# Reordering the opening of a fused conv and MLP kernel: half 1's conv shared differently between TensorE and VectorE, casts and transposes moved, a load held back

## The chip, the cores and the metric

One core of a Trainium2 chip runs the kernel. The metric is the device time of one execution in microseconds (us); lower is better. The kernel before took 698.84 us (median of 3, 698.34 to 699.54).

## The reference, cut to what matters

```python
# _attn_ref: x (8, 4096, 192), weight (8, 7)
w = softmax(weight, axis=-1)                       # 8 heads of 24 channels, 7 taps
out[b, s, h, g] = sum_k w[h, k] * x_pad[b, s + k, h, g]     # causal conv over the sequence
# _moe_ref: 32768 tokens
h = x @ w_in                                       # 192 -> 2048
g = np.maximum(0.01 * h, h)
return g @ w_out                                   # 2048 -> 192
```

## The kernel before

The tokens go through in blocks of 512 positions of two sequences. The first five blocks (NHALF) are done as two halves of 256 positions, the others whole. For each half: the conv makes `yt` (three chunks of 64 channels for both sequences), the first product `ph` is computed in units of two PSUM banks, ScalarE's leaky relu empties a unit into `g`, and the second product `po` follows a half later. The conv normally runs on VectorE, one multiply and six multiply-adds a chunk. At the start, when TensorE has nothing else to do, it does some chunks with diagonal matrices (`pe_conv_jobs`, 28 matmuls a chunk).

The first two blocks (halves 0 to 3) come by plain loads (`load_first`, float32), a cast, transposes on TensorE into PSUM and copies into `xt`. From block 2 on, casting loads and DMA transposes do this (`load_x`, `transpose_x`).

```python
    def cast_first(q, e, copy): ...        # x_nat -> x_bf, on the engine that is passed
    def transpose_first(q): ...            # 12 transposes on TensorE into two "po" PSUM buffers
    def evac_first(q, *copies): ...        # PSUM -> xt
    def conv_jobs(grp, chunks): ...        # VectorE: 7 instructions a chunk
    def pe_conv_jobs(grp, c): ...          # TensorE: 28 matmuls, and a scaling that empties them
    def mm1(grp, u): ...                   # one unit of ph, and its activation on ScalarE
```

The loop, with the opening's special cases:

```python
        for j in range(steps):
            for u in range(2 * j, 2 * j + 2):
                mm1(grp, u)
                if i == 0 and u == 1:
                    transpose_first(1)
                    evac_first(1, nc.vector.tensor_copy, nc.vector.tensor_copy)
                    ahead = conv_jobs(groups[1], range(NPEC, NCH))       # NPEC = 2
                    ...                                                  # two chunks for TensorE
                if i == 0 and u == 2:
                    for e in range(2):
                        cast_first(2, e, nc.scalar.copy)
                if i == 0 and u == 4:
                    transpose_first(2)
                    evacs[0](act_scale)
                if i == 0 and u in (3, 5):
                    for job in pe_ahead[: 4 * K]:
                        job()
                    ...
            for _ in range(quota):
                mm2_slot(slot)                                           # po
                slot += 1
            ...
```

Of the kernel before, what the change touches and what calls it, by code (L numbers as in the profile page):

```python
# [9 lines left out]
FP32 = mybir.dt.float32  # L10
BF16 = mybir.dt.bfloat16
# [3 lines left out]
def kernel(  # L15
# [8 lines left out]
    nc = tc.nc  # L24

    B, S, D = x.shape
    H, K = weight.shape
# [8 lines left out]
    NCH = D // CH  # L36
    ST = 512
    SUB = ST // 128
    HT = ST // 2
    HS = SUB // 2  # L40
    NFC = F // 128
# [5 lines left out]
    NPEC = 2  # L47
# [22 lines left out]
    def load_x(blk):  # L70

        if blk >= NBLK:
            return
        rp, st = divmod(blk, NB)
        t = xb_pool.tile([128, NCH, SUB, 2, CH], BF16, name="x_bf")
        src = x[:, st * ST : (st + 1) * ST, :].rearrange("r (s p) d -> r p s d", p=128)
        for c in range(NCH):
            for e in range(2):
                nc.gpsimd.dma_start(  # L79
                    out=t[:, c, :, e, :],  # L80
                    in_=src[2 * rp + e, :, :, c * CH : (c + 1) * CH],
                )
        x_bf[blk] = t

    def transpose_x(blk):

        if blk >= NBLK:
            return
        rp, st = divmod(blk, NB)
        if st == 0:  # L90
            new_xt(rp)
        t = x_bf.pop(blk)
        for c in range(NCH):
            nc.sync.dma_start_transpose(
                out=xt[rp][:, c, HALO + st * ST : HALO + (st + 1) * ST].rearrange(
                    "p (s k) -> p s k", s=SUB
                ),
                in_=t[:, c, :, :, :].rearrange("p s e k -> p (s e k)"),
            )
# [7 lines left out]
    def load_first(q, after=None):  # L107
        t = stage_pool.tile([128, 2, HS, D], FP32, name="x_nat")
        for e in range(2):
            ins = nc.sync.dma_start(  # L110
                out=t[:, e, :, :],
                in_=x[e, q * HT : (q + 1) * HT, :].rearrange("(c p) d -> p c d", p=128),
            )
            if after is not None and e == 0:
                tc.add_manual_dep(
                    ins.ins, after.ins.name,
                    mybir.DependencyInfo(
                        mybir.DependencyClass.Sync, mybir.DependencyReason.DATA
                    ),
                    reason="leave the DMA engines to w_in",  # L120
                )
        x_nat[q] = t

    def cast_first(q, e, copy):
        if q % 2 == 0 and e == 0:
            x_bf[q // 2] = xb_pool.tile([128, NCH, SUB, 2, CH], BF16, name="x_bf")
        h = q % 2
        copy(  # L128
            out=x_bf[q // 2][:, :, h * HS : (h + 1) * HS, e, :],
            in_=x_nat[q][:, e, :, :].rearrange("p s (c k) -> p c s k", c=NCH),  # L130
        )
# [20 lines left out]
    def evac_first(q, *copies):  # L152
        dst = xt[0][:, :, HALO + q * HT : HALO + (q + 1) * HT].rearrange(
            "p c (s i k) -> p i s c k", s=HS, i=2
        )
        for i, t in enumerate(ptr.pop(q)):
            copies[i](out=dst[:, i], in_=t)  # L157
# [4 lines left out]
    def conv_jobs(grp, chunks=range(NCH)):  # L162
        blk, t0, T = grp
        rp, st = divmod(blk, NB)
        if blk not in yt:
            yt[blk] = yt_pool.tile([128, NCH, ST], BF16, name="yt")
        y = yt[blk]
        jobs = []
        for c in chunks:
            for k in range(K):  # L170
                a = BASE + k + st * ST + t0
                src = xt[rp][:, c, a : a + T]
                dst = y[:, c, t0 : t0 + T]
                if k == 0:
                    jobs.append(
                        lambda s=src, d=dst, c=c: nc.vector.tensor_scalar_mul(  # L176
                            d, s, wk[:, c, 0:1]
                        )
                    )
                else:  # L180
                    jobs.append(
                        lambda s=src, d=dst, c=c, k=k: nc.vector.scalar_tensor_tensor(  # L182
                            out=d, in0=s, scalar=wk[:, c, k : k + 1], in1=d,
                            op0=mybir.AluOpType.mult, op1=mybir.AluOpType.add,
                        )
                    )
        return jobs
# [60 lines left out]
    def warm(n):  # L248
        for _ in range(n):
            nc.tensor.matmul(  # L250
                out=wa[:, 0, 0:HT], lhsT=zero[:, 0:128], rhs=zero, start=True, stop=True
            )
# [9 lines left out]
        out=w9[:, 0:K], in_=w9[:, 0:K], func=mybir.ActivationFunctionType.Exp,  # L262
        bias=nmax, scale=1.0, accum_out=w9[:, K : K + 1],
    )
    warm(7)
    wps = psum_h.tile([128, 2, ST], FP32, name="wps", tag="ph")
    for c in range(NCH):
        nc.tensor.matmul(  # L268
# [7 lines left out]
    cast_first(0, 1, nc.scalar.copy)  # L276

    wraw = wps[:, 0, 0 : NCH * (K + 1)].rearrange("p (c k) -> p c k", c=NCH)
    wkh = const_pool.tile([128, NCH, K], BF16, name="wkh")
    wkl = const_pool.tile([128, NCH, K], FP32, name="wkl")  # L280
    nc.vector.tensor_copy(out=wkh, in_=wraw[:, :, 0:K])
    nc.vector.tensor_sub(wkl, wraw[:, :, 0:K], wkh)


    diag = [const_pool.tile([128, 2, K, CH], BF16, name=f"diag{c}") for c in range(NPEC)]
# [14 lines left out]
        return act  # L300

    transpose_first(0)
    warm(3)
    diag_high(0)
    diag_low(0, range(2))
    evac_first(0, nc.vector.tensor_copy, nc.scalar.copy)
# [12 lines left out]
        )  # L319

    load_first(2, low)
    for job in conv_jobs(groups[0], range(NPEC, NCH)):
        job()
    for c in range(NPEC):
        pe_jobs, evac_y = pe_conv_jobs(groups[0], c)
        for job in pe_jobs:
            job()
        evac_y(act_scale)
        warm(3)
    cast_first(1, 0, nc.vector.tensor_copy)  # L330
    cast_first(1, 1, nc.vector.tensor_copy)
    load_first(3)
    load_x(2)
    transpose_x(2)


    g, po, osb, seal = {}, {}, {}, {}
# [70 lines left out]
    def evac_o(n):  # L408
# [7 lines left out]
        if n % 2 == 1:  # L416
# [3 lines left out]
                in_=osb.pop(n // 2),  # L420
            )

    slot, avail = 0, 0
    for i, grp in enumerate(groups):
        blk, t0, T = grp
        steps = T // 64
        if t0 == 0:
            g[blk] = g_pool.tile([128, NFC, 2, ST], BF16, name="g", tag="g")
        quota = (avail - slot) // steps

        if i == 0:
            ahead, pe_ahead = [], []
        elif i == 1:
            ahead = early[4:]
        else:
            ahead = conv_jobs(groups[i + 1]) if i + 1 < len(groups) else []
        per = -(-len(ahead) // (steps - 1)) if T == ST else -(-len(ahead) // steps)
        for j in range(steps):
            for u in range(2 * j, 2 * j + 2):
                mm1(grp, u)  # L440
                if i == 0 and u == 1:
                    transpose_first(1)
                    evac_first(1, nc.vector.tensor_copy, nc.vector.tensor_copy)
                    ahead = conv_jobs(groups[1], range(NPEC, NCH))
                    evacs = []
                    for c in range(NPEC):
                        pe_jobs, evac_y = pe_conv_jobs(groups[1], c)
                        pe_ahead += pe_jobs
                        evacs.append(evac_y)
                    per = len(ahead)  # L450
                if i == 0 and u == 2:
                    for e in range(2):
                        cast_first(2, e, nc.scalar.copy)
                if i == 0 and u == 4:
                    transpose_first(2)
                    evacs[0](act_scale)
                if i == 0 and u in (3, 5):
                    for job in pe_ahead[: 4 * K]:
                        job()
                    pe_ahead = pe_ahead[4 * K :]  # L460
                if i == 1 and u in (0, 2):
                    cast_first(3, u // 2, nc.scalar.copy)
            for _ in range(quota):
                mm2_slot(slot)
                slot += 1
            if i == 0 and j == 3:
                evac_first(2, nc.vector.tensor_copy, nc.vector.tensor_copy)
                early = conv_jobs(groups[2])
                for job in early[:4]:
                    job()  # L470
                evacs[1](nc.vector.tensor_scalar_mul)
            for job in ahead[per * j : per * (j + 1)]:
                job()
            if i == 1 and j == 1:
                transpose_first(3)
            if i == 1 and j == 3:
                evac_first(3, nc.vector.tensor_copy, nc.vector.tensor_copy)

            last_half = t0 + T == ST
            if j == steps // 4 and last_half:  # L480
                load_x(blk + 3)
            if j == steps // 2 and last_half and blk > 0:
                transpose_x(blk + 2)
        avail += 2 * T // 128 * NFC
# [37 lines left out]
```

## Time and profile before

| | kernel before |
|---|---|
| time | 698.84 us |
| span of the profiled execution | 696.4 us |
| TensorE (PE) busy | 689.5 us, 99% |
| VectorE (DVE), ScalarE (ACT) busy | 538.2 us, 513.3 us |
| first po matmul, from the span's start | 24.41 us |

A kernel whose TensorE is 99% busy can gain only where TensorE isn't in its steady beat, and that is the first 24 us. The prediction shows the lines.

### The profile page before, as it was taken

How to read it: one execution, taken by the hardware profiler on the slowest of the kernel's cores; microseconds unless marked ns; L12 is line 12 of the kernel's file. 1: busy time of each engine (PE TensorE's matmuls, PEld its weight loads, DVE VectorE, ACT ScalarE, POOL GpSimd, SP SyncE). 2: the span in 40 equal slices, each digit the busy share in tenths (PEclk: the TensorE clock that was granted, in tenths of full speed). 3: DMA queues.
4: the chain of work that ended last, by engine and by line, in shares of the span. 5: the costliest groups of instructions: out<-in, count | busy, mean ns of one | idle time of the engine just before them, and what ended most of it. 6: DMA issues, size and time to landing. Idle time of an engine off the chain costs nothing.

```text
span 696.4 us, 26058 instructions
## 1 busy us (share of the span) xinstructions
PE 689.5 (99%) x11786; PEld 612.7 (88%) x11786; DVE 538.2 (77%) x991; ACT 513.3 (74%) x579; POOL 142.1 (20%) x198
## 2 busy tenths in 40 slices
PE   8999999999999999999999999999999999999997
PEld 6899999678888888888888888888888888888887
DVE  6899999768777788777787777787777787777712
ACT  6888888977777777777777777777777777777770
POOL 6342221320122220222220222211222220000000
PEclk9999999999999999999999999999999999999999
DMA  9986553853556545556545556645556644122112
GB/s 173 127 98 76 82 80 77 88 78 73 76 65 92 82 70 81 74 66 93 81 69 81 73 69 93 79 67 85 66 76 88 86 71 72 53 52 59 47 37 69
DMA packets 184847, 54.39 MB, mean 78 GB/s; under 512 B 148384, under 2 KB 184736, under 8 KB 184736
## 3 DMA queue, kind: packets, MB, share of 16 engines
q0 software_dynamic: 98768, 14.17, 29.7%
q1 hardware_dynamic: 85968, 38.56, 23.1%
q8 instruction: 92, 1.51, 0.9%
q14 instruction: 19, 0.16, 0.1%
HBM read 29.88 MB, written 25.17 MB: 79 GB/s over the span
## 4 chain that ended last, share of the span: by engine, by line
PE 97%; DMA 1%; ACT 1%; POOL 0%; issue 0%; DVE 0%; SPq 0%; POOLq 0%; ACTq 0%
PE po L376 49%; PE ph L356 47%; DMA x_nat<-in_x_dram 1%; ACT g L363 1%; PE acc L201 0%; PE wps L268 0%; ACT diag L296 0%; POOL sel L228 0%; PE warm L250 0%; PE ptr L143 0%; ACT x_bf L128 0%; ACT xt L157 0%; POOL sel L226 0%; DVE o_sb L415 0%; POOL ident masks.py:199 0%
## 5 line engine op out<-in xcount | busy, mean ns | idle before, releaser
L363 ACT ACTIVATE g<-ph 128x1024 bf16<-128x1024 f32 x512 | 496.5, 1021 | 161.0 <-PE ph L356 161.0
L182 DVE SCALAR_TENSOR_TENSOR yt<-xt,wk,yt 128x512 bf16<-128x512 bf16 (+1 forms) x642 | 439.7, 685 | 17.4
L376 PE MATMUL po<-w_out,g 64*128 64x192 bf16 (+1 forms) x8048 | 398.1, 243 | 0.1
L376 PEld LDWEIGHTS <-g 64*128 64x128 bf16 (+1 forms) x8048 | 372.2, 94 | 28.8 <-ACT g L363 0.4
L356 PE MATMUL ph<-yt,w_in 64*128 64x512 bf16 (+1 forms) x3552 | 391.8, 347 | 1.6 <-ACT g L363 1.3
L356 PEld LDWEIGHTS <-w_in 64*128 64x128 bf16 x3552 | 249.9, 94 | 46.1 <-issue 5.0
L79 POOL DMA_DIRECT2D x_bf<-in_x_dram x180 | 133.7, 773 | 431.0 <-DMA xt<-x_bf 422.9
L415 DVE COPY o_sb<-po 128x192 f32<-128x192 f32 x216 | 77.2, 358 | 129.5 <-PE po L376 127.2
L176 DVE TENSOR_SCALAR yt<-xt,wk 128x512 bf16<-128x512 bf16 (+1 forms) x107 | 35.9, 336 | 1.0 <-DMA xt<-x_bf 0.8
L415 ACT COPY o_sb<-po 128x192 f32<-128x192 f32 x40 | 13.1, 327 | 0.0
L201 PE MATMUL acc<-xt,diag 64*64 64x256 bf16 x112 | 7.3, 280 | 0.0
L201 PEld LDWEIGHTS <-diag 64*64 64x64 bf16 x112 | 6.0, 111 | 1.2 <-issue 0.6
L250 PE MATMUL warm<-zero 128*128 128x256 bf16 x20 | 4.5, 373 | 1.1 <-DVE junk L218 1.1
L128 ACT CAST x_bf<-x_nat 128x384 bf16<-128x384 f32 x5 | 2.5, 507 | 3.6 <-DMA x_nat<-in_x_dram 3.6
L238 POOL DMA_DIRECT2D w_in<-in_moe_w_in_dram x8 | 5.1, 643 | 0.0
L157 DVE COPY xt<-ptr 128x384 bf16<-128x384 bf16 x7 | 2.2, 352 | 2.8 <-PE ptr L143 2.8
L250 PEld LDWEIGHTS <-zero 128*128 128x128 bf16 x20 | 2.0, 122 | 2.2 <-DVE junk L218 1.1
L296 ACT ACTIVATE diag<-ident,wkl 128x64 bf16<-128x64 bf16 x14 | 3.6, 339 | 0.0
L128 DVE CAST x_bf<-x_nat 128x384 bf16<-128x384 f32 x3 | 1.2, 439 | 1.4 <-DMA x_nat<-in_x_dram 1.4
L317 ACT ACTIVATE yt<-acc,rsum 128x256 bf16<-128x256 f32 x3 | 1.4, 470 | 1.2 <-PE acc L201 1.2
L143 PEld LDWEIGHTS <-x_bf 64*128 64x128 bf16 x48 | 1.2, 101 | 1.0 <-ACT x_bf L128 1.0
L268 PEld LDWEIGHTS wps<-w,sel 8*128 8x128 f32 x6 | 1.4, 322 | 0.7 <-POOL sel L228 0.7
(28 smaller groups left out, 12.5 us busy)
## 6 DMA issues: line engine op xcount, KB each, us to landing
out_dram<-o_sb SPq DMA_DIRECT2D x128, 192.0 KB, 2.1
x_bf<-in_x_dram POOLq DMA_DIRECT2D x180, 64.0 KB, 3.3
x_nat<-in_x_dram SPq DMA_DIRECT2D x8, 192.0 KB, 5.8
w_in<-in_moe_w_in_dram POOLq DMA_DIRECT2D x8, 192.0 KB, 7.8
xt<-x_bf SPq DMA_TRANSPOSE x90, 2.5
w_out<-in_moe_w_out_dram POOLq DMA_DIRECT2D x1, 768.0 KB, 14.2
w<-in_weight_dram SPq DMA_DIRECT2D x1, 0.2 KB
```

The costliest lines, as they stand in the source:

```text
L79: nc.gpsimd.dma_start(out=t[:, c, :, e, :], in_=src[2 * rp + e, :, :, c * CH : (c + 1) * CH],)
L128: copy(out=x_bf[q // 2][:, :, h * HS : (h + 1) * HS, e, :], in_=x_nat[q][:, e, :, :].rearrange("p s (c k) -> p c s k", c=NCH),)
L176: lambda s=src, d=dst, c=c: nc.vector.tensor_scalar_mul(d, s, wk[:, c, 0:1])
L182: lambda s=src, d=dst, c=c, k=k: nc.vector.scalar_tensor_tensor(out=d, in0=s, scalar=wk[:, c, k : k + 1], in1=d, op0=mybir.AluOpType.mult, ...
L201: lambda k=k, p=p, a=a, e=e, ps=ps: nc.tensor.matmul(out=acc[ps, :T], lhsT=diag[c][ps, p, k, :], rhs=xt[0][ps, c, a : a + T], start=(k == ...
L238: nc.gpsimd.dma_start(out=w_in[e * CH : (e + 1) * CH, :, fs], in_=moe_w_in[:, fs].rearrange("(c p) f -> p c f", p=CH),)
L250: nc.tensor.matmul(out=wa[:, 0, 0:HT], lhsT=zero[:, 0:128], rhs=zero, start=True, stop=True)
L296: act = nc.scalar.activation(out=diag[c][:, 1, k, :], in_=ident2, func=mybir.ActivationFunctionType.Copy, scale=wkl[:, c, k : k + 1],)
L356: nc.tensor.matmul(out=ph[:, e, i * T : (i + 1) * T], lhsT=w_in[ps, c, f * 128 : (f + 1) * 128], rhs=y[ps, c, t0 : t0 + T], start=(c == 0) ...
L363: act = nc.scalar.activation(out=g[blk][:, nf * u : nf * (u + 1), :, t0 : t0 + T], in_=ph.rearrange("p e (i t) -> p i e t", i=nf), func=my ...
L376: ins = nc.tensor.matmul(out=po[m], lhsT=g[b][ps, fc, e, s * 128 : (s + 1) * 128], rhs=w_out[ps, fc, :], start=(rt != 1 and fc == 0), stop ...
L415: copy(out=o_sb[:, n % 2, :], in_=po.pop(n))
```

## The change

The intent: take work off TensorE and ScalarE in half 0's row of units, where they hold each other up, and keep the DMA engines free for the weights. Half 1's conv goes one chunk to TensorE and two to VectorE; half 1's casts and transposes come ahead of the first ph matmul; half 2's casts go from ScalarE to VectorE and its transposes behind the eighth unit; half 3's copies come two steps earlier; block 2's loads wait for the end of half 0. The diff, cut (warm-up counts, shapes of two small tiles and removed lines are left out where `# ...` stands):

```diff
-    for job in conv_jobs(groups[0], range(NPEC, NCH)):
+    for n, job in enumerate(conv_jobs(groups[0], range(NPEC, NCH))):
+        if n in (4, 5):
+            cast_first(1, n - 4, nc.vector.tensor_copy)
         job()
+    load_first(3)
 # ...
-    cast_first(1, 0, nc.vector.tensor_copy)
-    cast_first(1, 1, nc.vector.tensor_copy)
-    load_first(3)
-    load_x(2)
-    transpose_x(2)
+    transpose_first(1)
+    evac_first(1, nc.vector.tensor_copy, nc.vector.tensor_copy)
 # ... in the loop:
+                if i == 0 and u == 0:
+                    pe_ahead, evac_y = pe_conv_jobs(groups[1], 0)
+                    ahead = conv_jobs(groups[1], range(1, NCH))
-                if i == 0 and u == 2:
-                    for e in range(2):
-                        cast_first(2, e, nc.scalar.copy)
-                if i == 0 and u == 4:
-                    transpose_first(2)
-                    evacs[0](act_scale)
-                if i == 0 and u in (3, 5):
-                    for job in pe_ahead[: 4 * K]:
+                if i == 0 and u == 3:
+                    for job in pe_ahead:
                         job()
 # ...
             if i == 0 and j == 3:
+                evac_y(nc.vector.tensor_scalar_mul)
+                for e in range(2):
+                    cast_first(2, e, nc.vector.tensor_copy)
+                transpose_first(2)
                 evac_first(2, nc.vector.tensor_copy, nc.vector.tensor_copy)
-                early = conv_jobs(groups[2])
-                for job in early[:4]:
-                    job()
-                evacs[1](nc.vector.tensor_scalar_mul)
+            if i == 1 and j == 1:
+                nc.gpsimd.tensor_copy(out=pjunk, in_=g[0][0:1, NFC - 1, 1, HT - 1 : HT])
+                load_x(2)
+            if i == 2 and j == 1:
+                transpose_x(2)
 # ...
             if i == 1 and j == 1:
                 transpose_first(3)
-            if i == 1 and j == 3:
                 evac_first(3, nc.vector.tensor_copy, nc.vector.tensor_copy)
```

More of the change, by code (lines that the diff above doesn't have):

```diff
@@ L264 @@
     )
-    warm(7)
+    warm(8)
     wps = psum_h.tile([128, 2, ST], FP32, name="wps", tag="ph")
@@ L278 @@
     wraw = wps[:, 0, 0 : NCH * (K + 1)].rearrange("p (c k) -> p c k", c=NCH)
-    wkh = const_pool.tile([128, NCH, K], BF16, name="wkh")
-    wkl = const_pool.tile([128, NCH, K], FP32, name="wkl")
-    nc.vector.tensor_copy(out=wkh, in_=wraw[:, :, 0:K])
-    nc.vector.tensor_sub(wkl, wraw[:, :, 0:K], wkh)
+    wkh = const_pool.tile([128, NPEC, K], BF16, name="wkh")
+    wkl = const_pool.tile([128, NPEC, K], FP32, name="wkl")
+    nc.vector.tensor_copy(out=wkh, in_=wraw[:, 0:NPEC, 0:K])
+    nc.vector.tensor_sub(wkl, wraw[:, 0:NPEC, 0:K], wkh)
     diag = [const_pool.tile([128, 2, K, CH], BF16, name=f"diag{c}") for c in range(NPEC)]
@@ L302 @@
     transpose_first(0)
-    warm(3)
+    warm(4)
     diag_high(0)
@@ L328 @@
         evac_y(act_scale)
-        warm(3)
-    cast_first(1, 0, nc.vector.tensor_copy)
-    cast_first(1, 1, nc.vector.tensor_copy)
-    load_first(3)
-    load_x(2)
-    transpose_x(2)
+        if c == 0:
+            warm(2)
+    transpose_first(1)
+    evac_first(1, nc.vector.tensor_copy, nc.vector.tensor_copy)
     g, po, osb, seal = {}, {}, {}, {}
@@ L421, in evac_o @@
             )
+    pjunk = const_pool.tile([1, 1], BF16)
     slot, avail = 0, 0
@@ L431 @@
         if i == 0:
-            ahead, pe_ahead = [], []
-        elif i == 1:
-            ahead = early[4:]
+            ahead = []
         else:
@@ L440 @@
                 mm1(grp, u)
-                if i == 0 and u == 1:
-                    transpose_first(1)
-                    evac_first(1, nc.vector.tensor_copy, nc.vector.tensor_copy)
-                    ahead = conv_jobs(groups[1], range(NPEC, NCH))
-                    evacs = []
-                    for c in range(NPEC):
-                        pe_jobs, evac_y = pe_conv_jobs(groups[1], c)
-                        pe_ahead += pe_jobs
-                        evacs.append(evac_y)
-                    per = len(ahead)
-                if i == 0 and u == 2:
-                    for e in range(2):
-                        cast_first(2, e, nc.scalar.copy)
-                if i == 0 and u == 4:
-                    transpose_first(2)
-                    evacs[0](act_scale)
-                if i == 0 and u in (3, 5):
-                    for job in pe_ahead[: 4 * K]:
+                if i == 0 and u == 0:
+                    pe_ahead, evac_y = pe_conv_jobs(groups[1], 0)
+                    ahead = conv_jobs(groups[1], range(1, NCH))
+                    per = len(ahead)
+                if i == 0 and u == 3:
+                    for job in pe_ahead:
                         job()
-                    pe_ahead = pe_ahead[4 * K :]
                 if i == 1 and u in (0, 2):
```

## The prediction

> **What bounds the kernel now.** I read the page's engine rows first, then the chain that ended last, then the timelines of the first 35 us engine by engine, because the diff touches nothing after the first three half blocks.
>
> ```profile
> PE 689.5 (99%) x11786; PEld 612.7 (88%) x11786; DVE 538.2 (77%) x991; ACT 513.3 (74%) x579; POOL 142.1 (20%) x198
> PE po L376 49%; PE ph L356 47%; DMA x_nat<-in_x_dram 1%; ACT g L363 1%; PE acc L201 0%; PE wps L268 0%; ACT diag L296 0%; POOL sel L228 0%; PE warm L250 0%; PE ptr L143 0%; ACT x_bf L128 0%; ACT xt L157 0%; POOL sel L226 0%; DVE o_sb L415 0%; POOL ident masks.py:199 0%
> ```
>
> TensorE (PE) is the bound: 99% busy, and 96% of the chain is the two products, ph (first) and po (second). From about 24 us on its timeline is one unbroken beat (24 ph matmuls, 32 po matmuls, 2.63 us a step). The change leaves these alone, so it can only move the moment at which the beat begins. That moment is the first po matmul, at 24.41 us:
>
> ```profile
> 10.67 0.50 PE L250 MATMUL warm<-zero 128*128 128x256 bf16 x3
> 11.11 1.58 PE L356 MATMUL ph<-yt,w_in 64*128 64x256 bf16 x24
> 12.51 0.35 PE L143 MATMUL ptr<-ident,x_bf 64*128 64x64 bf16 x12
> 13.14 1.75 PE L356 MATMUL ph<-yt,w_in 64*128 64x256 bf16 x24 [0.28 <-ACT g L363]
> 14.82 1.72 PE L201 MATMUL acc<-xt,diag 64*64 64x256 bf16 x28
> 16.47 0.83 PE L356 MATMUL ph<-yt,w_in 64*128 64x256 bf16 x12
> 17.57 0.35 PE L143 MATMUL ptr<-ident,x_bf 64*128 64x64 bf16 x12 [0.27 <-ACT x_bf L128]
> 18.48 0.83 PE L356 MATMUL ph<-yt,w_in 64*128 64x256 bf16 x12 [0.57 <-ACT g L363]
> 19.25 1.72 PE L201 MATMUL acc<-xt,diag 64*64 64x256 bf16 x28
> 20.90 1.48 PE L356 MATMUL ph<-yt,w_in 64*128 64x256 bf16 x24
> 22.85 1.75 PE L356 MATMUL ph<-yt,w_in 64*128 64x256 bf16 x24 [0.46 <-ACT g L363]
> 24.41 1.32 PE L376 MATMUL po<-w_out,g 64*128 64x192 bf16 x14
> ```
>
> Columns are start, length, engine, line. Between 11.11 and 22.85 PE does half 0's eight ph units (12 matmuls each), two transposes (ptr) and both conv chunks of half 1 (acc). The reader is to see that the units come in a halting row, although one takes only 0.66 us. Each is emptied by a ScalarE (ACT) activation of 1.02 us, and there are two ph buffers, so ACT sets the pace, and ACT is held up:
>
> ```profile
> 14.93 0.50 ACT L128 CAST x_bf<-x_nat 128x384 bf16<-128x384 f32 x1
> 17.00 0.51 ACT L128 CAST x_bf<-x_nat 128x384 bf16<-128x384 f32 x1 [1.57 <-DMA x_nat<-in_x_dram]
> 17.42 1.93 ACT L363 ACTIVATE g<-ph 128x1024 bf16<-128x1024 f32 x2
> 21.77 2.96 ACT L363 ACTIVATE g<-ph 128x1024 bf16<-128x1024 f32 x3 [1.15 <-PE ph L356]
> ```
>
> Half 2's two casts stand in ACT's order ahead of the fourth activation; the second waits 1.57 us for its load. The fourth activation, whose matmuls were issued by about 14.7, starts at 17.42. Later ACT waits 1.15 us for PE, which is then in the second conv chunk.
>
> **What the skill says.** "Perfetto Trace Analysis", section "Optimization Strategy", says to find the gaps on the bounding engine within a regime and ask which semaphore ends each; the reading above is that, and both gaps of 0.57 and 0.46 us end on ACT. "DMA: Bandwidth & Descriptors", section "Queues, rings and completion order", says that each DMA engine consumes the descriptors of a ring in order, and its section "Issuing engines are not separate DMA queues" that all issuers share the same 16 engines. The trace agrees: w_out was issued at 9.29 and took 14.2 us to land, at 23.5, behind the w_in copies (the last issued at 7.35, 11.3 us to landing, so 18.6), and the x copy waiting on its semaphore was released only then:
>
> ```profile
> 9.29 1.20 POOL L243 DMA_DIRECT2D w_out<-in_moe_w_out_dram x1 [1.31 <-DMA w_in<-in_moe_w_in_dram]
> 23.79 3.71 POOL L79 DMA_DIRECT2D x_bf<-in_x_dram x5 [3.88 <-DMA w_out<-in_moe_w_out_dram]
> ```
>
> "TensorE: Matmul & The Clock Gate", section "What's actually happening", says that the array runs at half clock until about 3.4 us of activity. The warm matmuls show it: seven take 1.67 us at 1.13, three take 0.50 at 8.58, although the clock row reads 9 throughout.
>
> **The change, part by part.**
>
> *Warm matmuls.* +1, +1, and 3+3 becomes 2. The eighth fits ahead of 3.00, where PE waits for POOL anyway. The fourth after the transposes delays the first conv by about 0.1 us (one cold matmul is 0.21, part of which comes back as warm ones later), and one fewer between the convs returns 0.11 (three take 0.33 start to start). Sum about 0.
>
> *Half 1's casts on VectorE (DVE), earlier.* They go between its conv steps from 7.70; a step is 0.52 start to start, a cast about 0.35 to 0.42. Half 1's loads have landed (in the kernel before, the casts at 10.71 show no wait). Casts done at about 10.3, DVE's chunk at 11.2 instead of 10.8. PE's second conv ends at about 10.6, transposes follow at once (0.3 us), and the first ph group needs chunk 1, which ACT delivers at 11.26 as before. So the first activation stays at about 12.1.
>
> *Transposes out of the ph row.* 0.35 us leave a place where PE waited for ACT anyway: no gain of its own.
>
> *Half 2's casts off ACT, onto DVE.* This removes the 1.57 us wait and two times 0.5 us from ACT. The fourth activation follows the third at 15.0 instead of 17.4.
>
> *One conv chunk of half 1 off PE.* 28 matmuls, 1.65 us start to start. It goes to DVE, where a chunk costs 3.4 us (13.54 to 16.95). DVE then does 11.2 copies, 11.9 and 15.2 two chunks, 18.5 scaling, 18.9 casts, done at 19.7. Half 2's transposes come after the eighth unit, on PE at about 20.1, so this fits.
>
> *The row.* Units 0 to 3 as now; conv 14.82; unit 4 at 16.47; unit 5 behind it at 17.1; unit 6 at 18.65, when unit 4 is emptied and the last w_in copy is in; unit 7 at 19.5; transposes 20.1; half 1's unit 0 at 20.7 and unit 1 at 21.65. PE would be ready for po at 22.3 instead of 24.41: 2.1 us.
>
> *w_out.* The first po needs it, and it landed at 23.5. The deferred x loads stood behind it in the ring, so taking them away moves it little, and x_nat moves the same bytes ahead of it. Then po starts at about 23.5 and the gain is 24.41 - 23.55 = 0.86 us. The other 1.2 us turn into a wait for w_out. Some DMA engines start x copies before the last w_out packet is through, so I allow 0.1 to 0.2 us for a quieter finish: 1.0 us.
>
> *DVE after that.* Half 2's conv (21 steps, 10.0 us, formerly begun at 18.6) now begins at 21.4; after 12 steps it waits for half 3's transposes (27.5), copies, and ends at about 32.9. PE needs it at 33.85 - 1.0 + 0.2 = 33.05. It just fits, and thereafter DVE needs 10.0 us a half against PE's 10.5.
>
> *Block 2's load and transposes.* Now gated on the end of half 0 and issued at about 39; needed by DVE at about 43; in the kernel before the first such transpose landed 4.5 us after issue under full load. Tight, behind a margin of 1 us.
>
> Sum: 698.84 - 1.0 = 697.9 us.
>
> **The rivals.**
>
> 1. *The whole 2.1 us arrive* (696.7). For: removing traffic might pull w_out in. Against: the ring order above; and DVE's half 2 conv, ending no earlier than about 32.5, would cap the gain near 1.5 (697.3).
> 2. *DVE becomes the bound of halves 2 and 3.* It takes on 3.4 us of conv and 0.8 of casts just where it has no slack. If its chain runs 0.5 us longer than I count, PE waits at 33; late transposes of block 2 would make it wait at 43. Cost up to 1 us: 698.8. For: margin only 0.1 to 0.3 us at 33; against: 0.5 us more slack with every half.
> 3. *Nothing changes*, because w_out slips: 698.8. Against: its bytes and its place in the ring are the same.
>
> **Range and chances.** All rivals lie between 696.7 and 699; runs of the kernel before spread over 1.2 us. I take 696.8 to 699.0. Two per cent is 14 us, more than the whole opening could give: faster 0.005, same 0.99, slower 0.005.
>
> **What would show it.** PE's longest wait turns from ACT into the w_out copy, 1 us or so just ahead of the first po, at about 23.5; ACT's activations of half 0 run without casts, the eighth over by about 21.6; half 1's first ph unit at about 20.7; half 2's first at about 32.9, with DVE's last step just before it. I am wrong if po starts well before 23 (w_out was helped), or if new DVE waits stand ahead of ph near 33 or 43.

## More of the kernel before

In the timeline of VectorE in the kernel before (start, length, engine, line, operation, count, and in brackets the idle time ahead of it and what ended it):

```profile
17.95 0.62 DVE L157 COPY xt<-ptr 128x384 bf16<-128x384 bf16 x2 [1.00 <-PE ptr L143]
18.61 0.29 DVE L176 TENSOR_SCALAR yt<-xt,wk 128x256 bf16<-128x256 bf16 x1
...
110.72 4.69 DVE L182 SCALAR_TENSOR_TENSOR yt<-xt,wk,yt 128x512 bf16<-128x512 bf16 x6
116.16 0.35 DVE L176 TENSOR_SCALAR yt<-xt,wk 128x512 bf16<-128x512 bf16 x1 [0.75 <-DMA xt<-x_bf]
```

Half 2's conv begins at 18.61. The last multiply-add of block 5, the first whole block, ends at 115.41 (110.72 + 4.69), and TensorE begins that block at 118.01:

```profile
118.01 1.48 PE L356 MATMUL ph<-yt,w_in 64*128 64x512 bf16 x12
```

VectorE is ahead: it then waits 0.75 us for a transpose of the next block.

## The result, and the profile after

The changed kernel took 698.31 us (median of 4, 698.09 to 698.45) against 698.78 (698.34 to 699.54) of the kernel before beside it; the ratio is 0.9992, 95% interval 0.9974 to 1.0009. A second set of five gave 699.01 (697.43 to 699.39) against 698.85 (698.04 to 699.34): 0.9996, interval 0.9984 to 1.0008. The two are the same within what can be told. (A ratio is the mean time of one kernel's runs over that of the other's of the same rounds, so not quite the ratio of the medians quoted.)

TensorE's timeline of the changed kernel, from the first ph matmuls on, and the one later line in which it stood still:

```profile
12.04 0.27 PE L357 MATMUL ph<-yt,w_in 64*128 64x256 bf16 x2
12.49 1.38 PE L357 MATMUL ph<-yt,w_in 64*128 64x256 bf16 x22 [0.18 <-ACT yt L317]
14.32 1.75 PE L357 MATMUL ph<-yt,w_in 64*128 64x256 bf16 x24 [0.46 <-ACT g L364]
16.00 1.72 PE L201 MATMUL acc<-xt,diag 64*64 64x256 bf16 x28
17.65 1.48 PE L357 MATMUL ph<-yt,w_in 64*128 64x256 bf16 x24
19.59 1.75 PE L357 MATMUL ph<-yt,w_in 64*128 64x256 bf16 x24 [0.46 <-ACT g L364]
21.16 0.35 PE L143 MATMUL ptr<-ident,x_bf 64*128 64x64 bf16 x12
21.54 1.75 PE L357 MATMUL ph<-yt,w_in 64*128 64x256 bf16 x24
23.99 1.31 PE L377 MATMUL po<-w_out,g 64*128 64x192 bf16 x14 [0.70 <-DMA w_out<-in_moe_w_out_dram]
...
118.99 1.04 PE L357 MATMUL ph<-yt,w_in 64*128 64x512 bf16 x8 [0.83 <-DVE yt L182]
```

The row of units now runs in pairs, and ScalarE's activations follow one another. TensorE is ready for po at 23.29 (23.99 - 0.70) although the row began 0.9 us later than before (12.04 against 11.11), and then waits for w_out. That is a gain of 0.42 us at the first po (24.41 - 23.99). At 118.99 it stands still once more: the first whole block waits 0.83 us for VectorE's conv. Matmul by matmul, TensorE is 0.49 us ahead of the kernel before until this point and 0.55 us behind after it. Two lines of the page of the changed kernel, the chain that ended last by engine and by line, say where the end now hangs:

```profile
PE 83%; DVE 12%; DMA 3%; issue 1%; POOL 0%; ACT 0%; POOLq 0%; ACTq 0%
PE po L377 43%; PE ph L357 40%; DVE yt L182 11%; DMA w_out<-in_moe_w_out_dram 2%; DVE yt L176 1%; DMA w_in<-in_moe_w_in_dram 1%; POOL sel L228 0%; ACT g L364 0%; DVE xt L157 0%; POOL sel L226 0%; DVE o_sb L416 0%; POOL ident masks.py:199 0%; PE ptr L143 0%; POOL ident masks.py:197 0%; POOLq masks.py:199 0%
```

Before, VectorE had 0% of the chain. Now it has 12%, about 84 us: the chain runs through the w_out copy, the first po, half 3's transposes and then VectorE's conv without a break up to block 5. In this view TensorE's wait itself is short; what shows is the work that it waited for. In VectorE's timeline of the changed kernel:

```profile
21.54 0.62 DVE L157 COPY xt<-ptr 128x384 bf16<-128x384 bf16 x2 [0.86 <-PE ptr L143]
22.19 0.29 DVE L176 TENSOR_SCALAR yt<-xt,wk 128x256 bf16<-128x256 bf16 x1
...
28.31 0.62 DVE L157 COPY xt<-ptr 128x384 bf16<-128x384 bf16 x2 [0.43 <-PE ptr L143]
...
114.25 4.69 DVE L182 SCALAR_TENSOR_TENSOR yt<-xt,wk,yt 128x512 bf16<-128x512 bf16 x6
```

Half 2's conv begins at 22.19 instead of 18.61, 3.58 us later, and block 5's ends at 118.94 instead of 115.41, 3.53 later. So VectorE's lateness is nearly that of half 2's conv, carried along for 97 us. On the way it waits once, 0.43 us at 28.31, for half 3's transposes, which follow the first po: there the late w_out holds up VectorE too.

### The profile page after: what moved, and what is told of

The parts are those of the page before. It is cut to its first block, busy times and chain, and to the rows that moved or that the text cites. A ratio compares the mean times of both kernels' runs of the same rounds, so it can differ in the third digit from the quotient of the medians.

```text
span 696.7 us, 26003 instructions
## 1 busy us (share of the span) xinstructions
PE 688.9 (99%) x11756; PEld 611.7 (88%) x11756; DVE 542.4 (78%) x1000; ACT 512.3 (74%) x576; POOL 142.2 (20%) x199
## 4 chain that ended last, share of the span: by engine, by line
PE 83%; DVE 12%; DMA 3%; issue 1%; POOL 0%; ACT 0%; POOLq 0%; ACTq 0%
PE po L377 43%; PE ph L357 40%; DVE yt L182 11%; DMA w_out<-in_moe_w_out_dram 2%; DVE yt L176 1%; DMA w_in<-in_moe_w_in_dram 1%; POOL sel L228 0%; ACT g L364 0%; DVE xt L157 0%; POOL sel L226 0%; DVE o_sb L416 0%; POOL ident masks.py:199 0%; PE ptr L143 0%; POOL ident masks.py:197 0%; POOLq masks.py:199 0%
## 5 line engine op out<-in xcount | busy, mean ns | idle before, releaser
L416 ACT COPY o_sb<-po 128x192 f32<-128x192 f32 x40 | 13.1, 327 | 0.0
```

What stands on the lines that cost most here:

```text
L416: copy(out=o_sb[:, n % 2, :], in_=po.pop(n))
```

## The experiments

Eleven runs were made, all correct; one is the changed kernel again. "First po", the waits and the start of half 2's conv are from each one's profiled execution, us from the span's start; "ratio" is to the kernel before of the same rounds; a row's median is of 5 executions (3 and 4 in the first two rows, 6 for the changed kernel with six blocks halved). The runs came in three calls, each on another chip, so two medians are to be compared only within a call: experiments 1 and 2 with the changed kernel of 3; experiments 4, 6, 7 and the last row; experiment 5 with the late load and the other kernel of 3.

| kernel | time, median (range) | ratio (95%) | first po | wait for w_out | half 2's conv begins | waits for VectorE later |
|---|---|---|---|---|---|---|
| before | 698.84 (698.34 to 699.54) | | 24.41 | 0 | 18.61 | 0 |
| changed | 698.31 (698.09 to 698.45) | 0.9992 (0.9974 to 1.0009) | 23.99 | 0.70 | 22.19 | 0.83 |
| changed, again | 699.01 (697.43 to 699.39) | 0.9996 (0.9984 to 1.0008) | 25.06 | 0.87 | 22.83 | 0.43 |
| changed + VectorE steps | 700.38 (699.51 to 701.26) | 1.0022 (1.0010 to 1.0034) | 25.04 | 0.83 | 22.86 | 1.45 and 1.08 |
| before + VectorE steps | 698.54 (698.35 to 699.35) | 0.9997 (0.9985 to 1.0009) | 24.78 | 0 | 19.19 | 0 |
| changed, six blocks halved | 698.03 (697.44 to 700.29) | 0.9996 (0.9984 to 1.0007) | 23.65 | 0.71 | 21.85 | 0 |
| before, six blocks halved | 698.26 (698.10 to 699.30) | 1.0000 (0.9987 to 1.0012) | 24.55 | 0 | 18.78 | 0 |
| changed, two chunks on TensorE | 698.63 (698.14 to 699.18) | 1.0000 (0.9988 to 1.0013) | 24.24 | 0 | 23.07 | 1.17 |
| before, half 2 late | 699.51 (698.98 to 700.21) | 1.0015 (1.0001 to 1.0029) | 24.80 | 0 | 23.64 | 0.50 and 0.51 |
| before, half 2's casts on VectorE | 698.24 (697.71 to 699.34) | 0.9996 (0.9983 to 1.0008) | 24.36 | 0 | 19.29 | 0 |
| changed, w_out in two copies | 697.76 (696.89 to 699.97) | 0.9993 (0.9980 to 1.0007) | 23.11 | 0 | 22.20 | 0.96 |
| changed, half 3's load late | 697.73 (697.08 to 698.12) | 0.9987 (0.9974 to 0.9999) | 22.30 | 0 | 21.39 | 1.18 |
| the last two ideas: late load, six halved | 696.72 (696.33 to 697.77) | 0.9977 (0.9963 to 0.9990) | 22.93 | 0 | 22.01 | 0 |

Two of the intervals only just miss 1 (0.9974 to 0.9999 and 1.0001 to 1.0029); among eleven that can be chance, so these two rest on their traces.

### 1. The changed kernel again

No edit.

> The changed kernel again, unaltered, for a tighter interval and a second profile. VectorE theory: the first po matmul starts about 0.4 us earlier than in the kernel before (24.0 against 24.41), and the first full block at about 118 us waits 0.8 us for VectorE's conv, so the time is within 0.1% of the kernel before (698.0 to 698.9). Rival, chance of one profile: the wait at 118 us is absent or differs by more than 0.5 us, and the time is 0.4 us below the kernel before. The slow phase of the array at the first conv (its first 28 matmuls took 3.19 us instead of 2.13) is either there again (an effect of the change) or not[...].

Measured: the wait at the first whole block is there again, 0.43 us, so it isn't chance. The first po came at 25.06, 1.1 us later than in the first profile, because w_out landed at 25.0 (issued at 9.4, 15.6 us to landing) instead of 23.95. TensorE waits for w_out in both. In this one its row had also waited 0.16 and 0.75 us for w_in, whose later copies came late as well (in the changed kernel of experiment 2 it is 0.69 and 0.76 us). The executions of this kernel spread over 2 us, and its start hangs on a landing time that varies.

The first conv on TensorE took 2.65 us here, 3.19 in the first profile, 2.13 in the kernel before. Over all thirteen profiles it took 2.05 to 3.19, and 3.14 in one of the kernel before with an edit far behind it. So the length of this slow phase of the array (its first microseconds, in which matmuls take longer) is not an effect of the change. It cost the first profile of the changed kernel about 1 us ahead of 12 us; without it TensorE would only have waited longer for w_out, which landed at 23.95.

### 2. More work for VectorE, in both kernels

The same edit to both: three multiply-adds of 0.787 us start to start on a scratch tile, near 36 us, where they touch nothing else. (The tile is made and cleared ahead of the loop: 0.48 us of VectorE near 11.7. It delays nothing that counts here: half 2's conv begins at 22.86, against 22.83 in experiment 1.)

```diff
             for job in ahead[per * j : per * (j + 1)]:
+            # ahead of this loop, in half 2's second step:
+            if i == 2 and j == 1:
+                for n in range(3):
+                    nc.vector.scalar_tensor_tensor(out=scr[:, 1], in0=scr[:, 0], scalar=wk[:, 0, 0:1],
+                                                   in1=scr[:, 1], op0=mult, op1=add)
```

> The changed kernel with three more VectorE steps of 0.787 us (2.36 us together, on a scratch tile) put in half 2's stretch, near 36 us. VectorE theory: VectorE has no slack left up to the first full block, so the whole 2.36 us come out: the wait there grows from 0.8 to about 3.2 us and the time by 2.3 us, to about 700.6. Rival, that only the start of the beat near 24 us counts: no change of time, 698.3.

> The kernel before with the same three VectorE steps (2.36 us). VectorE theory: there VectorE ends block 5's conv at 115.4 us and even waits 0.75 us for a transpose after it, while TensorE needs the last chunk at about 118.5, so about 3 us are free: no wait at 118 us, time unchanged (698.8, within 0.3). If VectorE were equally bound in both kernels, it would rise by 2.3 us.

Measured: the kernel before took them for nothing (0.9997, no wait). The changed kernel paid: in its timeline of TensorE,

```profile
46.77 1.27 PE L357 MATMUL ph<-yt,w_in 64*128 64x256 bf16 x20 [1.45 <-DVE yt L182]
121.91 1.04 PE L357 MATMUL ph<-yt,w_in 64*128 64x512 bf16 x8 [1.08 <-DVE yt L182]
```

The two waits are 2.53 us together, against 0.43 in the changed kernel of the same call, whose first po came at the same time (25.06 and 25.04). So 2.1 of 2.36 us came out, part of it already at half 3, and the profiled span grew by 2.3 us (699.6 against 697.3). The slack that VectorE had before is gone in the changed kernel. This is the clearest pair.

### 3. One more block in halves, in both kernels

```diff
-    NHALF = 5
+    NHALF = 6
```

> The changed kernel with six blocks instead of five done as two halves, so that VectorE gains two more halves of slack (about 0.5 us each) before it has to do a whole block's conv. VectorE theory: the wait of 0.83 us goes or falls under 0.1, and the time falls by 0.7 to 0.9 us, to about 697.5. Rival (the wait at the first full block comes from the switch of shape itself): the wait is as long, 20 us later, and the time stays at 698.3.

> Control: the kernel before with six blocks as halves instead of five. It has no wait for VectorE at the first full block, so there is nothing to gain: time unchanged, within 0.3 us of 698.7. If it falls by 0.8 us, six halves are faster in themselves, and what they brought to the changed kernel says nothing about VectorE.

Measured: in the changed kernel no wait for VectorE is left, neither at the old place nor at the new one. Its start is 0.76 us ahead of the kernel before and its end 0.64 us ahead: hardly anything is lost on the way. The control is flat: 1.0000. The timings of the changed one don't separate it (0.9996): its executions spread from 697.44, the one profiled, to 700.29, and why that one was long is not known. The time part of that expectation stays unproved by timing and rests on the trace. What the trace does show is that the wait comes from VectorE's lack of time and not from the switch of shape itself, which is still there at 138.24.

### 4. Two chunks of half 1 on TensorE again: a miss

```diff
-                    pe_ahead, evac_y = pe_conv_jobs(groups[1], 0)
-                    ahead = conv_jobs(groups[1], range(1, NCH))
+                    # jobs and scalings of chunks 0 and 1, as in the kernel before
+                    ahead = conv_jobs(groups[1], range(NPEC, NCH))
-                if i == 0 and u == 3:
+                if i == 0 and u in (3, 5):          # 28 matmuls each
 # ... both scalings where the one was
```

> The changed kernel with half 1's conv split as in the kernel before (two chunks on TensorE, one on VectorE), the rest of the change kept. VectorE theory: VectorE loses 3.4 us of conv and gains one scaling of 0.5, so the wait for it at the first full block (0.83 and 0.43 us in the two profiles) is 0. The second conv chunk costs TensorE 1.65 us in half 0's row, part of it where it waits anyway: ready for po at about 24.3 instead of 23.3, so the wait for w_out falls to between 0 and 0.7, by when w_out lands (23.5 to 25.0 in the profiles so far). Time 0.4 to 0.8 us below the changed kernel of the same kind of run, about 698.0. If the chunk on VectorE was a gain, this is slower.

Measured: the wait at the first whole block did not go; it rose to 1.17 us, and the time is that of the kernel before. So the first form of my reason, that the chunk given to VectorE is what it lacks later, is wrong. VectorE's timeline in this kernel shows why:

```profile
20.83 0.48 DVE L207 TENSOR_SCALAR yt<-acc,rsum 128x256 bf16<-128x256 f32 x1 [2.59 <-PE acc L201]
21.24 0.74 DVE L128 CAST x_bf<-x_nat 128x384 bf16<-128x384 f32 x2
22.42 0.62 DVE L157 COPY xt<-ptr 128x384 bf16<-128x384 bf16 x2 [0.44 <-PE ptr L143]
23.07 0.29 DVE L176 TENSOR_SCALAR yt<-xt,wk 128x256 bf16<-128x256 bf16 x1
```

The time saved on the chunk is spent idle: VectorE waits 2.59 us for TensorE's second chunk, and half 2's casts, transposes and copies stand behind that scaling in its order. Half 2's conv begins at 23.07, even later than in the changed kernel. What counts is when that conv begins, not how much VectorE was given ahead of it. The changed kernel shows the same in its own timeline above: VectorE stands idle for 0.86 us right ahead of half 2's copies, waiting for the transposes behind the eighth unit, so less conv there would not have let it begin earlier.

This gives a rough sum. From the first po to TensorE's need of the first whole block's last chunk it is about 94.2 us (in the changed kernel 118.16 - 23.99). From the start of half 2's conv to the end of block 5's it is about 96.8 (115.41 - 18.61 before, 118.94 - 22.19 after). VectorE's slack is (first po + 94.2) - (start + 96.8): before +3.2, changed -0.8 (measured wait 0.83), two chunks on TensorE -1.4 (1.17), half 2's casts on VectorE alone +2.5 (none). For the kernels with five blocks halved it gives the sign, but not always the size: for w_out in two copies and for half 3's load late it gives -1.7, and 0.96 and 1.18 were measured. The first term holds (94.2 in both), but the second varies from run to run, from 96.0 to 96.8: in these two kernels VectorE doesn't wait for half 3's transposes, and it needs 96.0 and 96.3.

### 5. Half 2's transposes late, alone, in the kernel before

```diff
                 if i == 0 and u == 4:
-                    transpose_first(2)
                     evacs[0](act_scale)
             if i == 0 and j == 3:
+                evacs[1](nc.vector.tensor_scalar_mul)
+                transpose_first(2)
                 evac_first(2, nc.vector.tensor_copy, nc.vector.tensor_copy)
                 # ... early steps of half 2's conv as before
-                evacs[1](nc.vector.tensor_scalar_mul)
             if i == 1 and j == 1:
                 transpose_first(3)
-            if i == 1 and j == 3:
                 evac_first(3, nc.vector.tensor_copy, nc.vector.tensor_copy)
```

The edit also puts the second chunk's scaling ahead of them, and half 3's copies two steps earlier. The trace tells these apart: the scaling was over at 21.88, and VectorE then waited 1.10 us for the transposes.

> The kernel before with one part of the change alone: half 2's transposes and copies placed after half 0's eighth unit (as in the change), and with them half 3's copies two steps earlier; both conv chunks of half 1 stay on TensorE and half 2's casts on ScalarE. Theory formed after the run with two chunks on TensorE: what counts at the first full block is when VectorE begins half 2's conv (18.6 us before, 22.2 changed, 23.1 with two chunks on TensorE), not how much conv it was given. So here, where it begins near 23.4, TensorE waits 0.6 to 1.3 us for VectorE at the first full block, and the time rises by as much, to about 699.6. Rival, that the added chunk is the cause: no wait there, 698.8.

Measured: 699.51 us, 1.0015 of the kernel before (interval 1.0001 to 1.0029). Three of the waits of TensorE in this kernel (waiter, what for, us in total, times, longest):

```profile
PE ph L356 <- ACT g L363: 2.0, 3, 1.4
PE ph L356 <- DVE yt L182: 0.5, 1, 0.5
PE po L376 <- DVE xt L157: 0.5, 1, 0.5
```

The wait for VectorE's conv, which the kernel before doesn't have, is there with both chunks on TensorE and no cast moved. By the sum above it should have been longer, 1.4 us from 24.80 and 23.64. But TensorE was late itself: it had waited 0.50 us more at a later po, whose PSUM buffers half 3's transposes held until VectorE had copied them. With these 0.50 counted the sum gives 0.9, and with the 96.4 us that VectorE needed in this run 0.5 to 0.6; measured was 0.51, a little under the 0.6 that was expected at least. So the place of half 2's transposes is enough to use up VectorE's slack. It is not all of this kernel's loss: the profiled execution ends 1.67 us behind the kernel before, of which 0.39 stand at the first po (TensorE, without the transposes to fill the gap, waits 1.40 us for ScalarE at 18.87), 0.60 come by 31 us and 0.68 at the first whole block. The reverse, the change with half 2's transposes at their old place, was not run.

### 6. Half 2's casts on VectorE, alone, in the kernel before

```diff
-                        cast_first(2, e, nc.scalar.copy)
+                        cast_first(2, e, nc.vector.tensor_copy)
```

> The kernel before with one part of the change alone: half 2's two casts on VectorE instead of ScalarE, nothing else moved. The fourth activation then starts near 15 us instead of 17.4 and half 0's fifth unit to eighth unit come 0.4 to 0.5 us earlier, first po near 24.0, unless w_out lands later. VectorE has 0.8 us more to do out of about 3 us of slack: no wait at the first full block. So this small part brings what the whole change brings: time 0.4 us below the kernel before (698.4). If the whole change is needed, it is the same as the kernel before.

Measured: 0.9996, interval 0.9983 to 1.0008, so it can't be told from the kernel before or from the changed one. The first po came at 24.36, not at 24.0. ScalarE was freed, but TensorE then waited 0.36 us for VectorE's cast, and the first conv took 2.72 us in this execution against 2.13, which shifts the row. No wait at the first whole block, as expected. Whether this small part brings any time stays open.

### 7. w_out in two copies

```diff
-    nc.gpsimd.dma_start(out=w_out, in_=moe_w_out.rearrange("(c p) d -> p c d", p=128))
+    for q in range(2):
+        cs = slice(q * NFC // 2, (q + 1) * NFC // 2)
+        nc.gpsimd.dma_start(out=w_out[:, cs, :],
+                            in_=moe_w_out.rearrange("(c p) d -> p c d", p=128)[:, cs, :])
```

> The changed kernel with w_out loaded by two copies of half the size. If the wait ahead of the first po is the copy's length (in-order ring), the first half is there at least 2 us earlier, the first eight po matmuls run without a wait, and the wait left is for the second half: under 0.3 us in place of 0.7 to 0.9, less what the eight matmuls take. VectorE theory: the beat starts 0.6 us earlier, but the wait for VectorE at the first full block grows by 0.2 to 0.6, so the time falls by no more than 0.4 us.

Measured: the halves landed 12.0 and 13.1 us after issue, at 21.7 and 23.8. TensorE's first po starts as soon as the ph matmuls ahead of it are through:

```profile
23.11 1.35 PE L382 MATMUL po<-w_out,g 64*128 64x192 bf16 x14
```

So it was the copy's last part that TensorE stood waiting for. The start is 1.30 us ahead of the kernel before, and the wait of 0.96 us at the first whole block takes most of that back, as expected: matmul by matmul the lead after it is 0.15 us. The timing (0.9993, range 696.89 to 699.97) doesn't separate them.

### 8. Half 3's load out of w_out's way, and both remedies together

```diff
-    load_first(3)
 # in mm1, at its end: return act
-                mm1(grp, u)
+                act_g = mm1(grp, u)
+                if i == 0 and u == 7:
+                    load_first(3, act_g)
-                if i == 1 and u in (0, 2):
-                    cast_first(3, u // 2, nc.scalar.copy)
+                if i == 1 and u in (1, 2):
+                    cast_first(3, u - 1, nc.scalar.copy)
```

> The changed kernel with half 3's load put behind half 0's last activation alone (five blocks as halves, as in the change). The wait for w_out goes (under 0.2 us) and the beat starts at 22.3 to 23.3, 0.7 to 1.7 us earlier than in the changed kernel, but VectorE, which begins half 2's conv at about 21.5 to 22.2 either way, is late at the first full block: wait of 1.2 to 2.0 us, time 0.3 to 0.6 us below the kernel before (698.2). If the VectorE wait doesn't grow, the time falls to 697.3.

> The changed kernel with both suspected waits taken away: half 3's load is issued only when half 0's last activation is done, which takes about 1.5 us of copies out of the way of w_out (half 3's casts follow one unit later), and six blocks as halves, so that VectorE has slack. Both theories: w_out lands at 22 to 23.5, the wait ahead of the first po is under 0.2, the beat starts at 22.5 to 23.4[...], no wait for VectorE at the first full block; VectorE may be waited for up to 0.4 us at half 2 or 3. Time 697.0, the fastest of all. If the time is at 698, something later takes the gain back.

Measured: half 3's load goes out at 21.63 instead of 10.73. With that alone w_out landed at 22.2, the first po came at 22.30 without a wait, 2.1 us ahead of the kernel before, and the wait for VectorE was 1.18 us. Time 697.73 us, 0.9987 (0.9974 to 0.9999). With six blocks in halves besides, the wait for VectorE is gone too; TensorE's timeline,

```profile
21.36 1.75 PE L356 MATMUL ph<-yt,w_in 64*128 64x256 bf16 x24
22.93 1.31 PE L377 MATMUL po<-w_out,g 64*128 64x192 bf16 x14
```

has no bracket at the first po and none later. The lead at the first po is 1.49 us and at the last 1.46: all of it reaches the end. The time is 696.72 us, 0.9977 (0.9963 to 0.9990) of the kernel before, the fastest. In this execution w_out landed at 22.3 and the first conv took 3.02 us; with a shorter slow phase, as in the other (2.39), the start could be up to 0.6 us earlier (an estimate, 22.93 - 22.3).

## Why the prediction was right or wrong

The predicted 697.9 us is 0.4 below the measured 698.31, and the range held it, as did "same". That is in part luck: the range is 2.2 us wide, the timings don't separate the change from no change, and of the 1.0 us forecast the profile has 0.42 at the first po and nothing at the end. Point by point:

- **The first product's row.** Right in kind: the halting went, ScalarE's fourth activation followed the third, and a gain at the first po stood against a wait for w_out. Off in size: I put TensorE ready for po at 22.3, and it was ready at 23.29. The term "Sum about 0" for the warm matmuls took the array's slow phase as fixed; the first conv took 3.19 us against 2.13, which experiment 1 shows to vary whatever the kernel. The wait for w_out covered it. The prediction's reading "the warm matmuls show it" is half right: they show two rates, but not 3.4 us, for the three at 5.78, begun 4.65 us after the first, still took 0.82 us against 0.50 at 8.58. In two of the eight profiles of the changed kernel and its variants the row also waited for w_in (0.91 and 1.45 us), which the prediction had in by 18.65; TensorE got the last of it at 20.5.
- **w_out.** Named as the new wait, and it was: 0.70 us. The mis-sized term is its landing, "at 23.5", with "0.1 to 0.2 us for a quieter finish": it landed at 23.95, 25.0, 25.0 and 23.6 in four profiles of the changed kernel and edits that hardly touch the opening. The gain at the first po was 0.42 us, not 1.0. That holding back block 2's loads would not bring it forward agrees (23.5 to 24.1 in five profiles of the kernel before and its variants), though no run held back these loads alone. What does move it is half 3's load, as experiment 8 shows: 22.2 and 22.3. "x_nat moves the same bytes ahead of it" was the clue, and I didn't draw it out; the change itself issues this load earlier (10.73 against 11.55), and whether that alone made w_out later was not tested.
- **DVE after that.** "It just fits, and thereafter DVE needs 10.0 us a half against PE's 10.5" is the step that failed. At 33 us it did fit, and each half did add slack. But after the tenth half comes a whole block, whose conv of 15.0 us (three times 4.99, from the starts at 103.89, 108.88, 113.86 and 118.86) has to be done within the last half of 10.5. The slack gained over the halves is used up there at once. Rival 2, VectorE as the bound, came true at 118 us and not at 33 or 43.
- **Its cause.** I counted "3.4 us of conv and 0.8 of casts" as what burdens VectorE. Experiment 4 speaks against the first: without the chunk the wait was longer. Experiment 5 shows what suffices: half 2's transposes, and with them its conv, placed behind the eighth unit.
- **Block 2's load and transposes.** Right: the first was issued at 39.5 and VectorE began on it at 43.55 without a wait. The margin is as small as was said: in experiment 1 the transpose was issued at 40.59, landed at 44.69, and VectorE stood 0.14 us for it.
- **The sum.** 0.42 gained at 24 us, 0.07 more by 30, then 1.04 lost at the first whole block (0.83 of it the wait itself, the rest how the two kernels run on from there). The profiled execution ends 0.28 us behind the kernel before; a hiccup of 0.27 us in that one at 304 us lies in between. The medians favour the change by 0.5 us in the first set and go against it by 0.2 in the second. Within this scatter the sign stays open, and the size of both waits doesn't.

## What to carry to other kernels

When a change moves work in an opening, follow the engine that takes it on up to the next change of shape, not only to the next wait: slack built up over uniform steps is spent at once where a step gets longer. Ask when each engine begins its unbroken run rather than how much it was given, because here a chunk of conv that took the place of idle time cost nothing, and transposes that stood in front of a long chain did. And where a start hangs on the last of a queue of copies, look for what can be issued behind it.

## What the Trainium skill lacked or had wrong

- "TensorE: Matmul & The Clock Gate", section "What's actually happening", says that the slow phase varies from run to run and costs under 1% of a typical span. That holds here, with numbers: the first conv took 2.05 to 3.19 us over thirteen executions, for the same 28 matmuls, starting 6.5 to 6.8 us into the span. What it lacks is that this can be more than a change is worth: it is 1.1 us, and the effect studied was 0.5. The page's 3.4 us of activity, which the prediction cites, is too short here: the first conv, begun at least 5.4 us after the first warm matmul (6.52 against 1.13), was slow in part or throughout in every profile, against 1.72 us for the second conv's 28 matmuls. The profile's clock row, which reads 9 all through, doesn't show it; it has to be read from the matmuls.
- "DMA: Bandwidth & Descriptors", section "Queues, rings and completion order": the order in a ring, which the page states of the queues of SyncE and ScalarE, agrees with the traces here for GpSimd's queue too (in the kernel before the last copy of w_in landed at 18.6 and w_out at 23.5). No page says how far the landing of such a copy scatters: w_out landed between 23.5 and 25.0 us over ten profiles in which nothing was moved out of its way or cut in two. Half 3's load, on another queue, made a difference to it (22.2 and 22.3 without that load ahead, or 12.5 and 13.5 us from issue against 13.9 to 15.6), which agrees with the section "Issuing engines are not separate DMA queues".
- No page that I read tells to look for a change of shape downstream of the stage that is edited: here 3.2 us of slack at 118 us were lost through a reordering at 20 us, and the profile's share of busy time for VectorE (77% before, 78% after) gave no hint of it.
